# Larger K and V transfers (4 MB items in 32 KB packets), a ring moved to the front of SBUF, regrouped wo loads and late bias loads in a cached-attention decode block

## The chip, the cores and the metric

The kernel runs on one core of a Trainium2 chip. Times are device microseconds of one execution.

The names in the profiles: PE is the matrix engine (PEld its weight loads), DVE the vector engine, ACT the scalar engine, POOL the general one; SP only issues transfers here. A q after a name is the engine's sequencer, which issues its instructions. Data come from the device's memory (HBM) into SBUF, the on-chip memory that the kernel addresses as 128 partitions, by 16 DMA engines (the trace has 16 landings for each item of the stream), in packets; PE writes its results to PSUM. A semaphore is a counter that the trace shows raised when an engine's work, or a transfer, is done.

## The reference, cut to what matters

One decode step for 2 sequences: an attention block with a KV cache, then an MLP, both scaled and shifted by factors computed from a condition c (adaLN). Nearly everything is reading: K and V caches of 2 x 4 x 32,768 x 128 bf16 are 134 MB of the 178 MB.

```python
mod = (_silu(c) @ w_mod).reshape(c.shape[0], 6, 1, -1)        # w_mod 1024 x 6144
sa, ca, ga, sb, cb, gb = ...
h = _layernorm(x) * (1 + ca) + sa
x = x + ga * _A_ref(h, K, V, wq, wo)      # 32 query heads, 4 KV heads, 32768 cached rows
h = _layernorm(x) * (1 + cb) + sb
x = x + gb * _B_ref(h, w1, b1, w2, b2)    # layernorm, 1024 -> 3584, gelu, 3584 -> 1024
```

## The kernel before

All large inputs go through one stream of DMAs, issued in a fixed order by the SP queue. Their target is a ring of 160 KB per partition. A new item may be issued when the items whose bytes it overwrites have been consumed. K and V come in items of 2 MB: 8,192 cache rows, so 64 rows or 16 KB for each of the 128 partitions. V runs five items behind K.

```python
CH_ROWS = 8192
TPC = CH_ROWS // 128          # 64 cache rows per partition and item
VLAG = 5
RING = 160 * 1024
...
    # about 44 KB per partition of small tensors are allocated first, the ring last
    arena = nc.alloc_sbuf_tensor("arena", [128, RING], mybir.dt.uint8)
    abase = nc.lookup_mloc(arena).addr
...
    def add(key, shape, src):                 # next place in the ring
        off = stream[-1].off + stream[-1].nbytes
        if off + nbytes > RING:
            off = 0
        it.view = nc.alloc_sbuf_tensor_at(..., [128] + list(shape), BF16, offset=abase + off)

    for k in range(8):  add(("wmod", k), [6 * DM], ...)       # 12 KB per partition
    for k in range(4):  add(("wq", k), [2, HQ * D], ...)      # 2 x 8 KB
    for n in range(NK + VLAG):
        if n < NK:
            add(("K", n), [TPC, D], kv_src(A_k_cache, ...))   # 16 KB
        v = n - VLAG
        if v >= 0:
            add(("V", v), [TPC, D], kv_src(A_v_cache, ...))
            if v % (2 * NCH) == 2 * NCH - 1:
                add(("wo", g), [8, DM], ...)                  # 16 KB, four of them
    for k in range(4):  add(("w1", k), [2, F], ...)           # 2 x 7 KB
    for k in range(4):  add(("w2", k), [hi - lo, 4 * DM], ...)  # 8 KB each

    def need(*key):                           # issue all items up to this one
        while pos[0] <= it.n:
            cur = stream[pos[0]]
            old = [o.reg for o in stream[:cur.n] if ...overlaps in the ring...]
            T.dma("sp", ..., writes=[cur.reg], frees=old)
```

PE transposes K in groups of 8 rows (`psKT`), DVE and ACT copy to `KT_sb`, PE forms scores and later multiplies V (`psO`). The biases b1 and b2 are loaded at the start from the ACT queue.

## Time and profile before

| | before |
|---|---|
| time, median (runs) | 431.43 us (431.33 to 431.49, 4 runs) |
| span of the profiled run | 429.7 us |
| bytes read | 178.28 MB |
| stream packets on each of the 16 DMA engines | 792, of which 512 are K and V |
| instruction fetches (packets of 16 KB) | 47 |

The page of before: busy time by engine, and the span in 40 slices with the DMA engines' busy share in tenths and the rate.

```profile
span 429.7 us, 12974 instructions
...
PE 292.2 (68%) x6035; PEld 258.2 (60%) x6035; DVE 162.5 (38%) x344; ACT 158.9 (37%) x266; POOL 1.3 (0%) x9
...
DMA  8999999999999999999999999999999999999992
GB/s 332 432 422 426 433 432 424 432 424 427 427 432 427 426 433 429 427 433 426 426 432 426 430 433 424 429 432 426 429 429 428 430 429 424 435 424 424 427 386 112
...
q1 hardware_dynamic: 14112, 178.27, 97.6%
q8 instruction: 47, 0.77, 0.6%
```

No compute engine is near full, and the DMA row is full. q1 is the stream, q8 the fetches of instructions. The chain of waits says the same in its shares of the span:

```profile
DMA 70%; PE 24%; ACT 2%; DVE 2%; issue 1%; SPq 1%; ACTq 0%
```

Now the tail: three windows (start and end in us, their length, busy time and count for each engine, the granted clock, the DMA share, GB/s).

```profile
380.00:410.00 30.00, 16.12 (x309) 12.48 (x310) 6.28 (x32) 1.69 (x3) 0.00 (x0) 0.50 1.01 425
410.00:418.00 8.00, 2.80 (x93) 2.63 (x90) 0.87 (x4) 0.25 (x1) 0.00 (x0) 0.50 0.94 396
418.00:424.00 6.00, 2.56 (x90) 2.48 (x91) 0.00 (x0) 0.00 (x0) 0.00 (x0) 0.50 0.50 208
```

From 418 us on exactly half of the DMA share remains. The landings explain it: the semaphore of an item is raised once by each of the 16 DMA engines, and the trace has each raise. These are the times in us after the first, worked out from the trace for the first and the last item:

```
wmod 0, first landing   6.31:  0  .08 .13 .14 .15 .16 .28 .29 .30 .30 .31 .32 .37 .38 .39 .40
w2 3,   first landing 416.68:  0  .22 .23 .24 .25 .99 1.73 2.84 7.06 7.11 8.53 8.56 8.67 8.70 8.79 9.01
```

Five engines are done at 417 us, three shortly after, and eight only after 423.7 us. The chain of waits in order of time (start, length, what) follows the last landing, at 425.69 us, and then four microseconds of tail:

```profile
396.29 29.40 DMA w<-in_B_w_dram
425.69 0.05 issue
425.74 1.03 PE psS L591 x32
```

A stream packet of 7 KB took 272 ns, of 8 KB 309 and of 16 KB 611, in nearly every case to the nanosecond. A fetch took 945 ns in the mean, and the first stream packet after it 1.09 us instead of 611 ns. So a fetch delays its DMA engine by about 945 + 480 ns, or 1.42 us (an estimate from these means). This is the step: six engines end about six steps late, two about five.

### The profile page before, as it was taken

How to read it: one execution, taken by the hardware profiler on the slowest of the kernel's cores; microseconds unless marked ns; L12 is line 12 of the kernel's file. 1: busy time of each engine (PE TensorE's matmuls, PEld its weight loads, DVE VectorE, ACT ScalarE, POOL GpSimd, SP SyncE). 2: the span in 40 equal slices, each digit the busy share in tenths (PEclk: the TensorE clock that was granted, in tenths of full speed). 3: DMA queues.
4: the chain of work that ended last, by engine and by line, in shares of the span. 5: the costliest groups of instructions: out<-in, count | busy, mean ns of one | idle time of the engine just before them, and what ended most of it. 6: DMA issues, size and time to landing. Idle time of an engine off the chain costs nothing.

```text
span 429.7 us, 12974 instructions
## 1 busy us (share of the span) xinstructions
PE 292.2 (68%) x6035; PEld 258.2 (60%) x6035; DVE 162.5 (38%) x344; ACT 158.9 (37%) x266; POOL 1.3 (0%) x9
## 2 busy tenths in 40 slices
PE   0643379859978764997877649777777697535553
PEld 0632379858867663896757548667666585203543
DVE  0200027545665332463543435445434454203200
ACT  1100016575574325362833534446436343500100
POOL 1000000000000000000000000000000000000000
PEclk9999999998989867696996959986988599555555
DMA  8999999999999999999999999999999999999992
GB/s 332 432 422 426 433 432 424 432 424 427 427 432 427 426 433 429 427 433 426 426 432 426 430 433 424 429 432 426 429 429 428 430 429 424 435 424 424 427 386 112
DMA packets 14500, 179.11 MB, mean 417 GB/s; under 512 B 1767, under 2 KB 1774, under 8 KB 2798
## 3 DMA queue, kind: packets, MB, share of 16 engines
q1 hardware_dynamic: 14112, 178.27, 97.6%
q8 instruction: 47, 0.77, 0.6%
q10 hardware_dynamic: 334, 0.02, 0.1%
q14 instruction: 7, 0.06, 0.0%
HBM read 178.28 MB, written 0.00 MB: 415 GB/s over the span
## 4 chain that ended last, share of the span: by engine, by line
DMA 70%; PE 24%; ACT 2%; DVE 2%; issue 1%; SPq 1%; ACTq 0%
DMA K<-in_A_k_cache_dram 50%; PE psKT L546 15%; DMA V<-in_A_v_cache_dram 9%; DMA w<-in_B_w_dram 7%; DMA wmod<-in_w_mod_dram 5%; PE psS L441 4%; PE psO L473 2%; PE psM L510 1%; ACT E_sb L462 1%; SPq L344 1%; PE psM L494 0%; DVE KT_sb L552 0%; PE psM L483 0%; ACT L462 0%; DVE msum L488 0%
## 5 line engine op out<-in xcount | busy, mean ns | idle before, releaser
L546 PE MATMUL psKT<-ident,K 128*128 128x128 bf16 x2048 | 181.1, 240 | 55.1 <-DMA K<-in_A_k_cache_dram 54.2
L546 PEld LDWEIGHTS psKT<-ident,K 128*128 128x128 bf16 x2048 | 138.2, 108 | 70.0 <-DMA K<-in_A_k_cache_dram 63.5
L550 ACT ACTIVATE KT_sb<-psKT 128x1024 bf16<-128x1024 bf16 x96 | 98.3, 1024 | 190.2 <-PE psKT L546 181.3
L552 DVE COPY KT_sb<-psKT 128x1024 bf16<-128x1024 bf16 x160 | 108.2, 689 | 137.7 <-PE psKT L546 137.0
L441 PE MATMUL psS<-qT,KT_sb 128*128 128x8 bf16 x2048 | 91.6, 168 | 7.2 <-ACT KT_sb L550 4.5
L441 PEld LDWEIGHTS psS<-qT,KT_sb 128*128 128x128 bf16 x2048 | 84.0, 100 | 8.6 <-ACT KT_sb L550 4.9
L473 PE MATMUL psO<-V,E_sb 128*32 128x512 bf16 x512 | 38.2, 424 | 10.1 <-DMA V<-in_A_v_cache_dram 9.5
L462 ACT ACTIVATE E_sb<-S_sb,negm 128x256 bf16<-128x256 f32 x64 | 32.5, 508 | 7.0 <-DVE negm L460 5.2
L447 DVE TENSOR_REDUCE m1c<-S_sb 128x8 f32<-128x512 f32 x32 | 22.0, 688 | 14.1 <-ACT S_sb L446 13.0
L473 PEld LDWEIGHTS psO<-V,E_sb 128*32 128x32 bf16 x512 | 11.5, 101 | 22.3 <-DMA V<-in_A_v_cache_dram 13.3
L446 ACT ACTIVATE S_sb<-psS 128x512 f32<-128x512 f32 x32 | 19.0, 594 | 4.4 <-PE psS L441 4.3
L418 PE MATMUL psS<-siluT,wmod 128*128 128x2 bf16 x384 | 11.2, 165 | 8.4 <-DMA wmod<-in_w_mod_dram 6.9
L418 PEld LDWEIGHTS psS<-siluT,wmod 128*128 128x128 bf16 x384 | 10.9, 104 | 8.8 <-DMA wmod<-in_w_mod_dram 7.3
L426 PE MATMUL psS<-hT,wq 128*128 128x2 bf16 x256 | 7.5, 165 | 12.5 <-DMA wq<-in_A_wq_dram 12.5
L426 PEld LDWEIGHTS psS<-hT,wq 128*128 128x128 bf16 x256 | 7.1, 104 | 12.8 <-DMA wq<-in_A_wq_dram 12.8
L591 PE MATMUL psS<-gT,w 128*128 128x2 bf16 x224 | 6.6, 165 | 9.2 <-DMA w<-in_B_w_dram 9.2
L395 ACT ACTIVATE stat<-stat 128x2 f32<-128x2 f32 x3 | 0.6, 203 | 31.8 <-DVE stat L394 31.8
L591 PEld LDWEIGHTS psS<-gT,w 128*128 128x128 bf16 x224 | 6.3, 104 | 9.5 <-DMA w<-in_B_w_dram 9.5
L462 ACT ACTIVATION_READ_ACCUMULATOR E_sb<-S_sb,negm 128x1 f32 x64 | 12.0, 187 | 0.0
L485 DVE RECIPROCAL rinv<-psM 128x1 f32<-128x1 f32 x8 | 1.3, 168 | 22.1 <-PE psM L483 22.1
L573 PE MATMUL psS<-h2T,w 128*128 128x2 bf16 x224 | 7.8, 172 | 2.5 <-DVE x1b L577 1.3
L573 PEld LDWEIGHTS psS<-h2T,w 128*128 128x128 bf16 x224 | 7.6, 118 | 2.6 <-issue 2.6
(86 smaller groups left out, 93.3 us busy)
## 6 DMA issues: line engine op xcount, KB each, us to landing
K<-in_A_k_cache_dram SPq DMA_DIRECT2D x32, 2048.0 KB, 44.2
V<-in_A_v_cache_dram SPq DMA_DIRECT2D x32, 2048.0 KB, 43.2
wmod<-in_w_mod_dram SPq DMA_DIRECT2D x8, 1536.0 KB, 17.2
wq<-in_A_wq_dram SPq DMA_DIRECT2D x4, 2048.0 KB, 37.7
wo<-in_A_wo_dram SPq DMA_DIRECT2D x4, 2048.0 KB, 43.0
w<-in_B_w_dram SPq DMA_DIRECT2D x4, 1792.0 KB, 41.8
w<-in_B_w_dram SPq DMA_DIRECT2D x3, 2048.0 KB, 31.0
w<-in_B_w_dram SPq DMA_DIRECT2D x1, 1024.0 KB, 29.4
```

Of the source, the lines that this page charges most:

```text
L418: pe(lambda e, w=it.view, j=j, k=k: e.matmul(psS[0][:, 2 * j:2 * j + 2], lhsT=w[:, j * 128:(j + 1) * 128], rhs=siluT[:, :, k], start=(k == ...
L426: pe(lambda e, w=it.view, h=h, k=k: e.matmul(psS[1][:, 2 * h:2 * h + 2], lhsT=w[:, k % 2, h * 128:(h + 1) * 128], rhs=hT[:, k, :], start=( ...
L441: pe(lambda e, t=t, jj=jj: e.matmul(ps[:, t * HPG:(t + 1) * HPG], lhsT=KT_sb[kn][:, jj, :], rhs=qT[:, b, g * HPG:(g + 1) * HPG], start=Tru ...
L446: act(lambda e: e.activation(Sc, ps[:, :].rearrange("p (t h) -> p h t", h=HPG), ACT.Copy), reads=[preg], writes=[f"S_sb{i % 2}_{cc}"])
L447: dve(lambda e: e.tensor_reduce(m1c[:, :, cc], Sc, AX.X, ALU.max), reads=[f"S_sb{i % 2}_{cc}"], writes=[f"m1c{cc}"])
L462: act(lambda e, h=h: e.activation(E_sb[j][:, :, h, :], S_sb[j][:, h, :].rearrange("p (u t) -> p u t", t=4), ACT.Exp, bias=negm[j][:, h:h + ...
L473: pe(lambda e, t4=t4, tg=tg, q=q: e.matmul(psO[32 * q:32 * q + 32, :], lhsT=E_sb[j][:, tg // 4, :, :].rearrange("p h t -> p (h t)"), rhs=i ...
L546: pe(lambda e, kq=kq, jj=jj, w=it.view, t=t: e.transpose(psKT[kq][:, jj * 128:(jj + 1) * 128], w[:, t, :], ident[:, :]), reads=[it.reg, "i ...
L550: act(lambda e, kn=kn, src=src: e.activation(KT_sb[kn][:, :, :], src, ACT.Copy), reads=[f"psKT{kq}"], writes=[f"KT_sb{kn}"])
L552: dve(lambda e, kn=kn, src=src: e.tensor_copy(KT_sb[kn][:, :, :], src), reads=[f"psKT{kq}"], writes=[f"KT_sb{kn}"])
L573: pe(lambda e, w=it.view, fc=fc, q=q, j=j, k=k: e.matmul(psS[0][:, 2 * fc:2 * fc + 2], lhsT=w[:, k % 2, q * 512 + j:(q + 1) * 512:4], rhs= ...
L591: pe(lambda e, w=it.view, q=q, j=j, k=k: e.matmul(psS[1][:, 2 * k:2 * k + 2], lhsT=w[:, q % 2, j * DM + k * 128:j * DM + (k + 1) * 128], r ...
```

## The change

The intent: fewer and larger packets and items for the same bytes, K and V in 4 MB items, whose 128 cache rows for each partition make one packet of 32 KB; "a 1 KB aligned ring"; wo in one item of 4 MB and two of 2 MB; b1 and b2 on the stream's own queue, late. The core of the diff (small consequences for counters, score buffers and schedule steps are cut):

```diff
-CH_ROWS = 8192
+CH_ROWS = 16384
-VLAG = 5
+STEPS = TPC // 8
+VLAG = 2
...
+    arena = nc.alloc_sbuf_tensor("arena", [128, RING], mybir.dt.uint8)
+    abase = nc.lookup_mloc(arena).addr
+    assert abase % 64 == 0
+
     ident = sb("ident", [128, 128], BF16)
...
-    arena = nc.alloc_sbuf_tensor("arena", [128, RING], mybir.dt.uint8)
-    abase = nc.lookup_mloc(arena).addr
...
-            if v % (2 * NCH) == 2 * NCH - 1:
-                g = v // (2 * NCH)
-                add(("wo", g), [8, DM], ...)
+            if v == 4 * NCH - 1:
+                add(("wo", 0), [2, 8, DM], ...)
+    for g in (2, 3):
+        add(("wo", g), [1, 8, DM], ...)
...
-    T.dma("act", ... b1m ...)
-    T.dma("act", ... b2m ...)
+    need("w1", 3)
+    T.dma("sp", ... b1m ...)          # transposed by PE after w1
+    need("w2", 2)
+    for lo, hi in ((0, 3), (3, 8)):
+        T.dma("sp", ... b2m[lo:hi] ...)   # transposed by PE before the last w2 part
```

Before, the ring starts at byte 61,440 of each partition, which is 60 x 1,024. After, it is allocated first and starts at 16,512: behind 128 bytes of constants, 128 past a multiple of 1 KB. The assertion only asks for a multiple of 64.

More of the change, by code (lines that the diff above doesn't have):

```diff
@@ L236, in bass_adaLN_cond__gqa_block_cached__mixer_channel_mlp__decode_kernel @@
     b1T = sb("b1T", [128, FT])
-    b2T = sb("b2T", [128, KT8])
     sgT = sb("sgT", [128, 2, KT8])
@@ L248, in bass_adaLN_cond__gqa_block_cached__mixer_channel_mlp__decode_kernel @@
     qT = sb("qT", [128, 2, HQ], BF16)
-    atT = [sb(f"atT{i}", [128, 8, 2], BF16) for i in range(2)]
+    atT = [sb(f"atT{i}", [128, 8, 2], BF16) for i in range(G)]
     msum = sb("msum", [128, 128])
@@ L263, in bass_adaLN_cond__gqa_block_cached__mixer_channel_mlp__decode_kernel @@
     res16 = sb("res16", [16, 128], BF16)
-    m1c = sb("m1c", [128, HPG, NCH])
+    m1c = sb("m1c", [128, HPG, NT // 64])
     m1 = sb("m1", [128, HPG])
@@ L322, in bass_adaLN_cond__gqa_block_cached__mixer_channel_mlp__decode_kernel @@
             add(("V", v), [TPC, D], kv_src(A_v_cache, v // NCH, v % NCH))
-            if v % (2 * NCH) == 2 * NCH - 1:
-                g = v // (2 * NCH)
-                add(("wo", g), [8, DM], A_wo[g * 1024:(g + 1) * 1024, :].rearrange("(p j) n -> p j n", j=8))
+            if v == 4 * NCH - 1:
+                add(("wo", 0), [2, 8, DM], A_wo[0:2048, :].rearrange("(g p j) n -> p g j n", g=2, j=8))
+    for g in (2, 3):
+        add(("wo", g), [1, 8, DM], A_wo[g * 1024:(g + 1) * 1024, :].rearrange("(g p j) n -> p g j n", g=1, j=8))
     for k in range(4):
@@ L339, in need @@
             old = [o.reg for o in stream[:cur.n] if o.off < cur.off + cur.nbytes and cur.off < o.off + o.nbytes]
-            if len(cur.view.shape) == 3:
-                dst = cur.view[:, :, :]
-            else:
-                dst = cur.view[:, :]
+            dst = cur.view[tuple(slice(None) for _ in cur.view.shape)]
             T.dma("sp", lambda e, dst=dst, src=cur.src: e.dma_start(dst, src), key=f"d_{cur.reg}", writes=[cur.reg], frees=old)
@@ L359, in bass_adaLN_cond__gqa_block_cached__mixer_channel_mlp__decode_kernel @@
     T.dma("act", lambda e: e.dma_start(x16[:, :], A_x.rearrange("b o (k p) -> (b o k) p", p=128)), key="ld_x", writes=["x16"])
-    T.dma("act", lambda e: e.dma_start(b1m[:, :], B_b1.rearrange("(q r) -> q r", r=512)), key="ld_b1", writes=["b1m"])
-    T.dma("act", lambda e: e.dma_start(b2m[:, :], B_b2.rearrange("(k p) -> k p", p=128)), key="ld_b2", writes=["b2m"])
     for t, nm in ((ident, "ident"), (identf, "identf")):
@@ L372, in bass_adaLN_cond__gqa_block_cached__mixer_channel_mlp__decode_kernel @@
     pe(lambda e: e.matmul(psM[:, 0:16], lhsT=x16[:, :], rhs=ident[0:16, 0:16], start=True, stop=True),
-       reads=["x16", "ident"], writes=["psM"], mark=False)
-    for j in range(4):
-        pe(lambda e, j=j: e.matmul(psM[:, 16 + 7 * j:23 + 7 * j], lhsT=b1m[:, j::4], rhs=ident[0:7, 0:7], start=True, stop=True),
-           reads=["b1m", "ident"], writes=["psM"], mark=False)
-    pe(lambda e: e.matmul(psM[:, 44:52], lhsT=b2m[:, :], rhs=ident[0:KT8, 0:KT8], start=True, stop=True),
-       reads=["b2m", "ident"], writes=["psM"])
+       reads=["x16", "ident"], writes=["psM"])
     dve(lambda e: e.tensor_copy(xT.rearrange("p k b -> p b k"), psM[:, 0:16].rearrange("p (b k) -> p b k", b=2)), reads=["psM"], writes=["xT"])
-    dve(lambda e: e.tensor_copy(b1T.rearrange("p (q j) -> p j q", j=4), psM[:, 16:44].rearrange("p (j q) -> p j q", j=4)), reads=["psM"], writes=["b1T"])
-    dve(lambda e: e.tensor_copy(b2T[:, :], psM[:, 44:52]), reads=["psM"], writes=["b2T"])
     def kb(ap2):
@@ L437, in qk @@
         b, g = i % 2, i // 2
-        ps, preg = psS[n % 2], f"psS{n % 2}"
+        hh, half = cc * (TPC // 64) + g8 // 8, (g8 // 8) % 2
+        ps, preg = psS[half], f"psS{half}"
         for jj in range(8):
-            t = g8 * 8 + jj
+            t = (g8 % 8) * 8 + jj
             pe(lambda e, t=t, jj=jj: e.matmul(ps[:, t * HPG:(t + 1) * HPG], lhsT=KT_sb[kn][:, jj, :], rhs=qT[:, b, g * HPG:(g + 1) * HPG],
@@ L443, in qk @@
                reads=[f"KT_sb{kn}", "qT"], writes=[preg], mark=(jj == 7))
-        if g8 == TPC // 8 - 1:
-            Sc = S_sb[i % 2][:, :, cc * TPC:(cc + 1) * TPC]
-            act(lambda e: e.activation(Sc, ps[:, :].rearrange("p (t h) -> p h t", h=HPG), ACT.Copy), reads=[preg], writes=[f"S_sb{i % 2}_{cc}"])
-            dve(lambda e: e.tensor_reduce(m1c[:, :, cc], Sc, AX.X, ALU.max), reads=[f"S_sb{i % 2}_{cc}"], writes=[f"m1c{cc}"])
+        if g8 % 8 == 7:
+            Sc = S_sb[i % 2][:, :, hh * 64:(hh + 1) * 64]
+            act(lambda e: e.activation(Sc, ps[:, :].rearrange("p (t h) -> p h t", h=HPG), ACT.Copy), reads=[preg], writes=[f"S_sb{i % 2}_{hh}"])
+            dve(lambda e: e.tensor_reduce(m1c[:, :, hh], Sc, AX.X, ALU.max), reads=[f"S_sb{i % 2}_{hh}"], writes=[f"m1c{hh}"])
     def softmax_1(i):
-        dve(lambda e: e.tensor_reduce(m1[:, :], m1c[:, :, :], AX.X, ALU.max), reads=[f"m1c{cc}" for cc in range(NCH)], writes=["m1"])
+        dve(lambda e: e.tensor_reduce(m1[:, :], m1c[:, :, :], AX.X, ALU.max), reads=[f"m1c{hh}" for hh in range(NT // 64)], writes=["m1"])
     def softmax_2(i):
@@ L463, in softmax_3 @@
                                             accum_out=rowsum[j][:, h:h + 1]),
-                reads=[f"S_sb{j}_{cc}" for cc in range(NCH)] + [f"negm{j}"], writes=[f"E_sb{j}", f"rowsum{j}"])
+                reads=[f"S_sb{j}_{hh}" for hh in range(NT // 64)] + [f"negm{j}"], writes=[f"E_sb{j}", f"rowsum{j}"])
     def pv(v):
@@ L492, in extract_2 @@
         b, g = i % 2, i // 2
-        at = atT[g % 2]
+        at = atT[g]
         pe(lambda e: e.matmul(psM[:, 256:384], lhsT=hmat.rearrange("p h e -> p (h e)"), rhs=msum[:, :], start=True, stop=True),
@@ L502, in red @@
                 return e.tensor_reduce(at[:, :, b], pick.rearrange("p e j -> p j e"), AX.X, ALU.add)
-        dve(red, reads=["pick"], writes=[f"atT{g % 2}_{b}"])
+        dve(red, reads=["pick"], writes=[f"atT{g}_{b}"])
     def wo(g):
-        it = need("wo", g)
-        at = atT[g % 2]
+        it, gg = (need("wo", 0), g) if g < 2 else (need("wo", g), 0)
+        at = atT[g]
         for j in range(8):
             for k in range(KT8):
-                pe(lambda e, j=j, k=k: e.matmul(psM[:, 400 + 2 * k:402 + 2 * k], lhsT=it.view[:, j, k * 128:(k + 1) * 128], rhs=at[:, j, :],
+                pe(lambda e, j=j, k=k: e.matmul(psM[:, 400 + 2 * k:402 + 2 * k], lhsT=it.view[:, gg, j, k * 128:(k + 1) * 128], rhs=at[:, j, :],
                                                 start=(j == 0 and k == 0), stop=(j == 7), skip_group_check=True),
-                   reads=[it.reg, f"atT{g % 2}_0", f"atT{g % 2}_1"], writes=["psM"], mark=(j == 7 and k == KT8 - 1))
+                   reads=[it.reg, f"atT{g}_0", f"atT{g}_1"], writes=["psM"], mark=(j == 7 and k == KT8 - 1))
         pv_ = psM[:, 400:416].rearrange("p (k b) -> p k b", b=2)
@@ L532, in bass_adaLN_cond__gqa_block_cached__mixer_channel_mlp__decode_kernel @@
         at(n + 1, 2, lambda i=i: extract_2(i))
-        if i % 2:
-            at(n + 1, 6, lambda i=i: wo(i // 2))
+        if i == 3:
+            at(n + 1, 6, lambda: wo(0))
+            at(n + 1, 8, lambda: wo(1))
+        elif i == 5:
+            at(NK + VLAG, 5, lambda: wo(2))
+        elif i == 7:
+            at(n + 1, 6, lambda: wo(3))
     for n in range(NK + VLAG + 1):
-        for g8 in range(TPC // 8):
+        for g8 in range(STEPS):
             if n < NK:
@@ L567, in bass_adaLN_cond__gqa_block_cached__mixer_channel_mlp__decode_kernel @@
     dve(lambda e: e.tensor_copy(h2T[:, :, :], xc[:, :, :]), reads=["xc"], writes=["h2T"])
+    need("w1", 3)
+    T.dma("sp", lambda e: e.dma_start(b1m[:, :], B_b1.rearrange("(q r) -> q r", r=512)), key="ld_b1", writes=["b1m"])
     for k in range(KT8):
@@ L576, in bass_adaLN_cond__gqa_block_cached__mixer_channel_mlp__decode_kernel @@
                reads=[it.reg, "h2T"], writes=["psS0"], mark=(fc == FT - 1))
-    dve(lambda e: e.tensor_tensor(x1b[:, :, :], mod(5), b2T[:, :].unsqueeze(2).to_broadcast([128, KT8, 2]), ALU.mult), reads=["modT", "b2T"], writes=["x1b"])
-    dve(lambda e: e.tensor_tensor(x1b[:, :, :], x1b[:, :, :], x1T[:, :, :], ALU.add), reads=["x1b", "x1T"], writes=["x1b"])
+    for j in range(4):
+        pe(lambda e, j=j: e.matmul(psM[:, 16 + 7 * j:23 + 7 * j], lhsT=b1m[:, j::4], rhs=ident[0:7, 0:7], start=True, stop=True),
+           reads=["b1m", "ident"], writes=["psM"], mark=(j == 3))
+    dve(lambda e: e.tensor_copy(b1T.rearrange("p (q j) -> p j q", j=4), psM[:, 16:44].rearrange("p (j q) -> p j q", j=4)), reads=["psM"], writes=["b1T"])
     dve(lambda e: e.tensor_tensor(zT[:, :, :], psS[0][:, 0:2 * FT].rearrange("p (f b) -> p f b", b=2), b1T[:, :].unsqueeze(2).to_broadcast([128, FT, 2]), ALU.add),
@@ L585, in bass_adaLN_cond__gqa_block_cached__mixer_channel_mlp__decode_kernel @@
     dve(lambda e: e.tensor_tensor(gT[:, :, :], sg[:, :, :], zT[:, :, :], ALU.mult), reads=["sg", "zT"], writes=["gT"])
+    need("w2", 2)
+    b2_v = B_b2.rearrange("(k p) -> k p", p=128)
+    for lo, hi in ((0, 3), (3, 8)):
+        T.dma("sp", lambda e, lo=lo, hi=hi: e.dma_start(b2m[lo:hi, :], b2_v[lo:hi, :]), key=f"ld_b2_{lo}", writes=[f"b2m_{lo}"])
+    need("w2", 3)
     for q in range(7):
         it = need("w2", q // 2)
+        if q == 6:
+            pe(lambda e: e.matmul(psM[:, 44:52], lhsT=b2m[:, :], rhs=ident[0:KT8, 0:KT8], start=True, stop=True),
+               reads=["b2m_0", "b2m_3", "ident"], writes=["psM"])
+            dve(lambda e: e.tensor_tensor(x1b[:, :, :], mod(5), psM[:, 44:52].unsqueeze(2).to_broadcast([128, KT8, 2]), ALU.mult),
+                reads=["modT", "psM"], writes=["x1b"])
+            dve(lambda e: e.tensor_tensor(x1b[:, :, :], x1b[:, :, :], x1T[:, :, :], ALU.add), reads=["x1b", "x1T"], writes=["x1b"])
         for j in range(4):
```

## The prediction

> **What bounds the kernel now.** The DMA stream. The page: span 429.7 us, 178.3 MB read, DMA at 9 tenths in nearly all 40 slices, 422 to 435 GB/s in the middle; PE is busy for 68%, DVE 38%, ACT 37%. The chain of waits is 70% DMA. By the issue and landing times, 12 to 19 MB are queued ahead at every issue after the start: the stream never starves, and the SP queue's waits on PE (197 us) are only the ring being full.
>
> The averages hide a second part. The windows of the tail give a DMA share of 0.94 for 410 to 418 us and 0.5 from 418 to 424. The 16 landings of one item lie 0.4 us apart for the first item and 9.0 us for the last: some engines finish 9 us late. The lag grows in steps of about 1.42 us that go with the 47 instruction-fetch packets of 16 KB (945 ns each, and the next stream packet takes about 1.1 us instead of 611 ns). Six engines collect six such steps. These end the kernel: last landing 425.7 us, then 4 us of tail.
>
> **What the change does to that.**
> 1. 32 KB packets: K and V go from 512 packets on each engine to 256. On the leading engine, 2 MB items of 16 packets (wq, w2) land 4.88 to 4.90 us apart, those of 8 packets (K, V) 4.86: about 3.4 ns per packet. [...] 256 fewer: 0.9 us.
> 2. 33 fewer items: 33 fewer semaphore packets on each engine, 9 ns each: 0.3 us.
> 3. Instruction fetches: the same 6,013 PE instructions are built, so the same fetches and lag. [...] Gain 0; here nearly 9 us stay.
> 4. b1 and b2 leave the start. Their packets take 18 and 46 ns on at most 8 engines, and the lag at 14 us is still under 0.5 us: gain 0. Late, they hide beside waits for w2: cost 0.
> 5. Ring: five 4 MB slots instead of ten of 2 MB. K0 lands 5 us later and slots come free later, but even when PE runs behind (11 to 14 us for 4 MB of K), nearly 4 items (about 39 us) stay queued. Cost 0.
> 6. wo 2 and 3 come after all of V; wo 3 lands where it did. LayerNorm, w1 and GELU end about 1 us before w2 lands; this stays.
> 7. Alignment: as built, the ring starts at byte 61,440 (a multiple of 1 KB) before and 16,512 (128 bytes past one) after. No gain; a loss of 0 to 2 us is possible.
>
> **Predicted time.** 431.4 - 1.2 = 430.2 us, range 428.7 to 431.8. Chances: faster by over 2%: 0.02; within 2%: 0.96; slower: 0.02.
>
> **What would show each step.** 4,096 packets of 32 KB, about 1,213 ns each, in place of 8,192 of 16 KB. Leading-engine landings 9.69 us apart per 4 MB, not 2 x 4.86. Still 47 fetches, a spread of about 9 us at the end, and half the DMA share in the last 8 us. At least 8 MB ahead at each issue; no middle slice under 420 GB/s.
>
> **What would make it wrong.** A fetch between 32 KB packets that costs much more or less than 1.42 us (six times on the late engines); a penalty of the new ring address; slower HBM reads with partition rows 32 KB apart; a starved queue in the K-only beginning, where PE falls behind.

The sum is 0.9 us (step 1) and 0.3 us (step 2), 1.2 us in all, and 0 for the other steps.

## The result, and the profile after

| | before | after |
|---|---|---|
| time, median | 431.43 us (431.33 to 431.49, 4 runs) | 432.75 us (432.70 to 432.88, 4 runs) |
| ratio | | 1.0031 (95%: 1.0014 to 1.0049) |
| span of the profiled run | 429.7 us | 430.9 us |
| first and last landing of the last item | 416.68, 425.69 us | 417.21, 427.00 us |

A ratio is the mean time of one kernel's runs over that of the other's runs of the same rounds, so it is not quite the ratio of the medians. Executions over 1.5% slower than the fastest of the same kernel are left out of the means.

The change makes the kernel slower by 0.3%. That lies within 2%, but outside the predicted range and on the other side of the kernel before. The page after, and the chain's shares:

```profile
span 430.9 us, 12949 instructions
...
PE 286.8 (67%) x6035; PEld 257.1 (60%) x6035; DVE 161.2 (37%) x343; ACT 157.5 (37%) x266; POOL 1.3 (0%) x9
...
DMA  8999999999999999999999999999999999999982
GB/s 330 428 421 420 439 433 433 423 425 429 431 424 429 421 432 438 430 432 424 422 424 427 440 435 420 427 423 433 433 432 424 428 428 426 424 416 418 419 367 113
...
q1 hardware_dynamic: 9518, 178.27, 97.2%
q8 instruction: 47, 0.77, 0.7%
...
DMA 65%; PE 26%; ACT 4%; DVE 2%; issue 1%; SPq 1%; DVEq 0%; ACTq 0%
```

4,594 packets are gone from q1 and the stream is still full: its bound has not moved. The number of fetches is the same, 47, but their share rose from 0.6 to 0.7%. The three windows of the tail:

```profile
380.00:410.00 30.00, 16.90 (x367) 13.34 (x360) 6.21 (x31) 1.69 (x3) 0.00 (x0) 0.61 1.01 419
410.00:418.00 8.00, 3.87 (x122) 3.69 (x119) 1.07 (x5) 0.25 (x1) 0.00 (x0) 0.50 0.96 397
418.00:424.00 6.00, 1.87 (x64) 1.79 (x64) 0.00 (x0) 0.00 (x0) 0.00 (x0) 0.50 0.54 224
```

From 380 to 410 us, where wo, w1 and w2 run in both kernels with the same packets, the rate fell from 425 to 419 GB/s at the same DMA share of 1.01. No engine starved: the packets got longer. The chain's end is the same, 1.3 us later:

```profile
398.35 28.65 DMA w<-in_B_w_dram
427.00 0.05 issue
427.04 1.03 PE psS L602 x32
```

The single packets show what happened. Means in ns, without those that follow a fetch; the spread is the last minus the first of the 16 landings of the last item:

| | ring at | 7 KB | 8 KB | 16 KB | 32 KB | fetch | spread, us |
|---|---|---|---|---|---|---|---|
| before | 61,440 | 272.0 | 309.0 | 611.0 | | 945 | 9.01 |
| after | 16,512 | 276.0 | 313.3 | 614.7 | 1,216.5 | 1,066 | 9.78 |

Packets of 7, 8 and 16 KB take about 4 ns longer, those of w1 and w2 too, which the change did not touch. The 12 KB packets of wmod, the first of the stream, take only 1.4 ns longer in the mean (461.8 against 460.3), and the first half of them are not longer at all. Fetches take 0.12 us longer in the mean, even the first two (1,059 ns; before 932 and 929), which run beside 12 KB packets of wmod before any 32 KB packet exists. That spoke against the packet size and for the ring's address, but one trace of a change with four parts does not show it.

### The profile page after: what moved, and what is told of

The parts are those of the page before. It is cut to its first block, busy times and chain, and to the rows that moved or that the text cites. A ratio compares the mean times of both kernels' runs of the same rounds, so it can differ in the third digit from the quotient of the medians.

```text
span 430.9 us, 12949 instructions
## 1 busy us (share of the span) xinstructions
PE 286.8 (67%) x6035; PEld 257.1 (60%) x6035; DVE 161.2 (37%) x343; ACT 157.5 (37%) x266; POOL 1.3 (0%) x9
## 4 chain that ended last, share of the span: by engine, by line
DMA 65%; PE 26%; ACT 4%; DVE 2%; issue 1%; SPq 1%; DVEq 0%; ACTq 0%
DMA K<-in_A_k_cache_dram 45%; PE psKT L542 16%; DMA wo<-in_A_wo_dram 9%; DMA w<-in_B_w_dram 7%; DMA wmod<-in_w_mod_dram 5%; PE psS L432 5%; ACT E_sb L453 3%; PE psO L464 2%; PE psM L501 1%; DVE KT_sb L548 1%; SPq L343 1%; ACT KT_sb L546 1%; PE psM L485 1%; PE psM L474 1%; PE psM L444 0%
## 5 line engine op out<-in xcount | busy, mean ns | idle before, releaser
L542 PE MATMUL psKT<-ident,K 128*128 128x128 bf16 x2048 | 178.2, 238 | 45.1 <-DMA K<-in_A_k_cache_dram 43.7
L542 PEld LDWEIGHTS psKT<-ident,K 128*128 128x128 bf16 x2048 | 136.0, 107 | 53.9 <-DMA K<-in_A_k_cache_dram 46.8
L464 PE MATMUL psO<-V,E_sb 128*32 128x512 bf16 x512 | 34.7, 417 | 6.6 <-ACT E_sb L453 5.5
L464 PEld LDWEIGHTS psO<-V,E_sb 128*32 128x32 bf16 x512 | 13.2, 104 | 21.2 <-issue 10.9
L501 PE MATMUL psM<-atT,wo 128*128 128x2 bf16 x256 | 7.1, 164 | 3.7 <-DMA wo<-in_A_wo_dram 3.7
L501 PEld LDWEIGHTS psM<-atT,wo 128*128 128x128 bf16 x256 | 6.9, 99 | 3.9 <-DMA wo<-in_A_wo_dram 3.9
```

The lines of the kernel that those rows point to most:

```text
L464: pe(lambda e, t4=t4, tg=tg, q=q: e.matmul(psO[32 * q:32 * q + 32, :], lhsT=E_sb[j][:, tg // 4, :, :].rearrange("p h t -> p (h t)"), rhs=i ...
L501: pe(lambda e, j=j, k=k: e.matmul(psM[:, 400 + 2 * k:402 + 2 * k], lhsT=it.view[:, gg, j, k * 128:(k + 1) * 128], rhs=at[:, j, :], start=( ...
L542: pe(lambda e, kq=kq, jj=jj, w=it.view, t=t: e.transpose(psKT[kq][:, jj * 128:(jj + 1) * 128], w[:, t, :], ident[:, :]), reads=[it.reg, "i ...
```

## The experiments

Three theories. **A**: the ring's address, 128 bytes past a multiple of 1 KB, makes every packet and every fetch dearer, and the larger packets are in themselves a gain. **B**: larger packets or items make a fetch dearer. **C**: the regrouped wo and the late b1 and b2 cost the time. All runs passed the check of their results (which let an omission in e3 pass, see there); the tables give medians, and the kernel before as it ran in the same rounds.

### e1: the kernel before with its ring 128 bytes further

```diff
     # the kernel before, nothing else changed
+    nc.alloc_sbuf_tensor("ring_pad", [128, 128], mybir.dt.uint8)
     arena = nc.alloc_sbuf_tensor("arena", [128, RING], mybir.dt.uint8)
```

Expected: 

> The kernel before with nothing changed but 128 bytes of padding ahead of the ring, so that it starts at 61,568, 128 bytes past a multiple of 1 KB. Theory A (ring address): every stream packet gets about 3 to 5 ns longer (7 KB packets from 272 to about 277 ns in the mean, 16 KB from 611 to about 614 in the median), a fetch goes from 945 to about 1,066 ns, the final spread from 9.0 to about 9.9 us, and the time rises by 2.5 to 3.5 us to 434 to 435 us (about 3 ns on 1,050 packets of each engine, and 6 x 0.15 us of fetches). Theory B (32 KB packets or larger items make a fetch dearer): no change, 431.4 us, fetch 945 ns. Theory C (wo regrouped, b1 and b2 late cost the time): no change.

Measured: 435.19 us against 431.42 us, ratio 1.0087 (1.0073 to 1.0101). Packets of 7 KB 276.1 ns, of 16 KB 614.3 ns, fetches 1,065 ns, spread 9.78 us. The window that fell from 425 to 419 GB/s in the change reads the same here:

```profile
380.00:410.00 30.00, 15.69 (x261) 10.69 (x253) 6.29 (x32) 1.69 (x3) 0.00 (x0) 0.50 1.00 419
```

So 128 bytes of padding alone, with packets, items and program unchanged, give both marks of the change and cost 3.8 us, a little more than the 2.5 to 3.5 us expected. B and C are refuted as causes of these two marks. The last item's first landing is 2.87 us later, over 792 packets 3.6 ns for each; the spread adds 0.77 us.

### e2: the change with its ring on a multiple of 1 KB

```diff
     # the kernel after
+    nc.alloc_sbuf_tensor("ring_pad", [128, 896], mybir.dt.uint8)
     arena = nc.alloc_sbuf_tensor("arena", [128, RING], mybir.dt.uint8)     # now at 17,408
```

Expected: 

> The kernel after with 896 bytes of padding ahead of the ring, which then starts at 17,408, a multiple of 1 KB. Theory A: packets of 7 KB back at 272 ns and of 32 KB at 1,213 ns, fetch back at 945 ns, spread about 9.0 us, time about 430.2 us, my prediction for the change without an alignment cost. Theory B: packets back at their length, but fetch still 1,066 ns and spread 9.9 us: about 431.1 us. Theory C: 432.7 us as after, less what shorter packets give.

Measured: 429.90 us (429.80 to 430.17), ratio to before 0.9966 (0.9953 to 0.998). Packets are back at 272, 309 and 611 ns, those of 32 KB take 1,213 ns, a fetch 936 ns, the spread is 8.92 us.

```profile
span 428.1 us, 12949 instructions
```

and its windows of the tail:

```profile
380.00:410.00 30.00, 17.08 (x400) 14.78 (x400) 6.83 (x34) 1.69 (x3) 0.00 (x0) 0.61 1.01 425
410.00:418.00 8.00, 3.04 (x107) 2.96 (x108) 0.45 (x3) 0.25 (x1) 0.00 (x0) 0.50 0.86 359
418.00:424.00 6.00, 2.69 (x92) 2.50 (x89) 0.16 (x1) 0.00 (x0) 0.00 (x0) 0.50 0.45 187
```

The rate in the first window is 425 GB/s again. The intended version beats both kernels: 1.5 us under before and 2.85 us under the change as it was built. (The kernel after ran in other rounds; by the ratios to before, 1.0031 and 0.9966, the difference is 2.8 us.) 2.85 us agrees with the trace: the last landing comes at 424.19 instead of 427.00 us, of which the first landing makes 1.95 us (536 packets, again 3.6 ns each) and the spread 0.86 us, most of which is six fetches of 0.13 us each.

### e3: e2 with K and V in 2 MB items again

```diff
     # e2
-CH_ROWS = 16384
+CH_ROWS = 8192
-VLAG = 2
+VLAG = 5
```

(and the score buffer chosen by the item's number again).

Expected: 

> As e2, with K and V again in 2 MB items of 16 KB packets (ten slots, V five items behind), so that of the change only the wo grouping, the late b1 and b2 and the moved tensors remain. Theory A: within 0.3 us of before, 431.4 us, and 1.2 us slower than e2. Theory B: fetch back at 945 ns only here, time 431.4 us and equal to or faster than e2. Theory C: over 431.4 us, by what wo, b1 and b2 cost.

Measured: 431.41 us, ratio to before 0.9998 (0.9986 to 1.0011); fetch 931 ns.

One thing is wrong with this run, and the check of the results did not notice it. The change puts the product with the second wo group at step 8 of an item. An item of 2 MB has only steps 0 to 7, so in e3 this product is never computed, although its weights are loaded. The trace shows three products of 64 matmuls instead of four (e2 first, then e3):

```profile
L502 PE MATMUL psM<-atT,wo x256: 163/163/185, 260.2 to 391.6; 128*128 128x2 bf16 x128
L502 PE MATMUL psM<-atT,wo x192: 163/165/187, 261.2 to 392.9; 128*128 128x2 bf16 x192
```

That takes 64 matmuls out of the middle, and one fetch (46 in place of 47). The bytes and transfers are complete, and the last item's eight late landings come in the same steps as before (7.07 and 7.23 us, six from 8.56 to 8.69), so the omission should not have moved the end; a run with the fourth product was not made.

With this reserve, what remains of the change, wo regrouped, b1 and b2 late, tensors moved, is worth nothing that these runs can tell. e2, which computes everything, says the same: of its 1.52 us under before, the closer landings of K and V explain 1.4 (worked out in the point on steps 1 and 2). C falls, and B too: with 2 MB items (e3) and with 4 MB items (e2) a fetch costs the same. e3 minus e2 is what the large items are worth: 1.51 us.

### e4, e5, e6: how much alignment it takes

The kernel before with 64, 256 and 512 bytes of padding ahead of its ring, otherwise as e1.

Expected of 64 bytes: 

> The kernel before with 64 bytes of padding ahead of the ring (61,504). If only the remainder by some power of two counts, whether 256, 512 or 1,024: the same loss as with 128 bytes, fetch about 1,066 ns, 435 us. If the loss grows with the distance: half of it, about 433.3 us. If 64 bytes are alignment enough: 431.4 us and fetch 945 ns.

Expected of 256 bytes: 

> The same with 256 bytes (61,696). If a multiple of 256 is enough: 431.4 us, 7 KB packets 272 ns, fetch 945 ns. If 512 or 1,024 is needed: about 435 us as with 128 bytes.

Expected of 512 bytes: 

> The same with 512 bytes (61,952). If a multiple of 512 is enough: 431.4 us, fetch 945 ns. If 1,024 is needed: about 435 us.

| padding | ring start modulo 256 | time, us | before, us | ratio (95%) | 7 KB packet, ns | fetch, ns |
|---|---|---|---|---|---|---|
| 64 (e4) | 64 | 435.35 | 431.31 | 1.0094 (1.0078 to 1.0111) | 276.3 | 1,076 |
| 128 (e1) | 128 | 435.19 | 431.42 | 1.0087 (1.0073 to 1.0101) | 276.1 | 1,065 |
| 256 (e5) | 0 | 431.35 | 431.31 | 1.0001 (0.9987 to 1.0016) | 272.0 | 936 |
| 512 (e6) | 0 | 431.41 | 431.31 | 1.0005 (0.999 to 1.002) | 272.0 | 931 |

Here a ring on a multiple of 256 lost nothing (e5, e6), one 64 or 128 bytes past it lost 0.9% (e4, e1), and between these two the loss doesn't grow with the distance (4.04 and 3.77 us). The assertion in the change would pass in each of the four cases.

### e8: the smallest repair of the change

```diff
     # the kernel after; the ring then starts at 16,640 = 65 x 256
+    nc.alloc_sbuf_tensor("ring_pad", [128, 128], mybir.dt.uint8)
```

Expected: 

> The kernel after with only 128 bytes of padding, so that the ring starts at 16,640, a multiple of 256 but not of 512. If a multiple of 256 is all that is needed, with 32 KB packets too: as e2, 429.9 us, 32 KB packets 1,213 ns, fetch about 940 ns. If the large packets need 1 KB: over 431 us.

Measured: 430.11 us (before 431.39 us, ratio 0.997, 0.9955 to 0.9985), 32 KB packets 1,213 ns, fetch 943 ns. So 256 is enough for the large packets too, which took 1,216.5 ns at 16,512.

### e7: six more fetches, a test that failed

The sums above rest on the reading that the late engines are late because of instruction fetches. To test it, I added useless matmuls among those of wq, each of them two PE instructions (a weight load and a multiply); they write unused PSUM.

```diff
     # e2, in the wq loop, eight times
+        for r in range(96):
+            pe(lambda e: e.matmul(psM[:, 500:502], lhsT=ident[:, :], rhs=hT[:, 0, :], start=True, stop=True), ...)
```

Expected: 

> e2 (the change on a 1 KB aligned ring) with 768 useless small matmuls among those of wq, where PE has time; they write an unused part of PSUM and the result stays right. They are 1,536 more PE instructions, 6 more fetches (53 in place of 47). If the lag of the late engines is made of fetches, and the late engines end the kernel: half of the late engines get one more step, spread from 8.9 to about 10.3 us, time from 429.9 to about 431.3 us. If the lag has another cause, or PE's fetches do not end the kernel: no change, 429.9 us.

Measured: 437.30 us (before 431.31 us), 53 fetches, but a spread of 7.38 us. The test was not clean. The matmuls took more time than I had reckoned: K began at 84.4 us instead of 63.2 us, PE freed the ring's slots late, and the stream ran empty.

```profile
100.00:120.00 20.00, 16.77 (x390) 16.04 (x387) 12.34 (x22) 12.75 (x21) 0.00 (x0) 1.00 1.00 418
120.00:140.00 20.00, 16.99 (x364) 15.16 (x368) 10.48 (x16) 12.18 (x20) 0.00 (x0) 0.83 0.68 279
```

The DMA share of 0.68 in the second window is the gap. While the stream waited, the late engines caught up (the spread fell from 3.3 us to about 0.5 us for all but one), so the end says nothing of fetches. It does show how much room the five-slot ring has: PE 21 us late in the K-only beginning is too much.

### e9: three more fetches, in PE's idle time

Half as many useless matmuls, 32 after each wmod item and 16 after each half of a wq item.

Expected: 

> e2 with 384 useless small matmuls (half of e7), 32 after each wmod item and 16 after each half wq item, so that K starts as in e2 (at about 63 us; in e7 it started 21 us late and the ring ran empty). 768 more PE instructions, 3 more fetches (50). If fetches make the lag and the late engines end the kernel: one to three engines get a seventh step, spread from 8.9 to about 10.3 us, time from 429.9 to about 431.3 us. If not: 429.9 us and spread 8.9 us.

Measured: 431.24 us (431.14 to 431.30; before 431.39 us in these rounds, 431.42 us in those of e2), 50 fetches: 768 instructions made three more, one for each 256, as 1,536 made six in e7. K began at 63.2 us as in e2, and the stream stayed full.

```profile
q8 instruction: 50, 0.82, 0.7%
```

The landings of the last item in us after the first:

```
e2, first 415.26:  0 .14 .18 .30 .31 .32 2.26 3.07  7.14 7.46  8.54 8.59 8.71 8.82 8.84  8.92
e9, first 415.48:  0 .04 .09 .10 .13 .30 1.74 2.45  8.28 8.45  8.46 8.47 8.50 8.60 8.67  9.98
```

The two engines with five steps got their sixth, and one with six its seventh. This one alone ends the kernel: the last landing is 1.27 us later (0.22 in the first landing, 1.06 in the spread) and the time 1.34 us, about one step. e2 ran on another chip; against e8, which differs from e2 only in the padding and ran in the same rounds as e9, it is 1.13 us. So fetches make the lag, and the latest engine sets the time. The packet records name no DMA engine; that the fetches fall on eight of the 16 in turn is read from these landings, and from the fetches' durations, which repeat in eights: before, 932, 929, 967, 968, 947, 886, 881, 941 ns, then 933, 921, 962, 961, 949, 886, 886, 941.

## Why the prediction was wrong, point by point

- **Step 7, alignment, is the step that failed.** It said: "No gain; a loss of 0 to 2 us is possible." Measured, the loss is 2.85 us (432.75 us as built, 429.90 us in e2 with only the padding changed; 2.64 us against e8). I had read both addresses from the builds, and then left the term out of the sum: 430.2 us is the time without it, and the upper end of 431.8 us did not even hold the 2 us that the step itself allowed. Those 2 us were a guess: no run had moved the ring yet.
- **Step 3, fetches: "Gain 0".** It took the cost of a fetch to be unaffected by the change, which no run had shown. True for the packets' size: with 32 KB packets on an aligned ring a fetch takes 936 ns (931 to 945 beside 16 KB in e3, e5, e6 and before) and the spread is 8.92 us (e2). Not true for the address: 1,066 ns, and 0.86 us more at the end. This is about 0.3 of the loss, and I had not thought of any link between the ring's address and fetches.
- **Steps 1 and 2, the gain of larger packets and fewer semaphores,** were right in direction and somewhat small: 1.2 us estimated, 1.51 us measured between e3 and e2, 1.52 us between before and e2. The landings of K and V on the leading engine (the first of the 16 to finish an item) are 9.68 us apart per 4 MB in e2, against 2 x 4.863 us before: about 0.044 us less, 32 times, or 1.4 us. I had forecast 9.69. The kernel after, with its longer packets, has 9.71. The runs show the gain of fewer packets and fewer semaphores in sum alone, not each by itself.
- **Step 4, b1 and b2, and step 6, wo:** 0, as predicted, as far as the runs can tell. e3, which keeps their transfers, is within 0.02% of before, but lacks one of the four wo products; e2 has them all and leaves 0.1 us that the landings of K and V don't explain.
- **Step 5, the ring:** at least 8.4 MB were queued ahead at each issue after the first few, as predicted under the marks (8), but that is two items and at most about 20 us of transfers, not the "nearly 4 items (about 39 us)" of the step itself: it fell so low at five issues, first at 105.8 us. The stream did not starve, and the middle slices stay at 420 GB/s or more. (Single slices are a rough mark: some of e2 read 416 too. The windows of the tail are the better one.) e7 shows that the room is not large.
- Of the predicted marks, the 4,096 packets of 32 KB, the 47 fetches and the half share at the end came true; the time of a packet (1,213 ns) came true only in e2.

In one sum, in us: 431.4 (before) - 1.5 (large items) + 2.85 (ring address) = 432.75. It closes by construction, since both terms are differences to e2; what supports it from outside is that e1, without large items, shows the same 3.6 ns per packet and nearly the same growth of the spread.

Not settled: why a destination off a multiple of 256 lengthens packets of 7 to 32 KB by about 4 ns (3.5 to 4.3) whatever their size, but the first 12 KB packets of wmod not at all, and why it lengthens a fetch (945 to 1,066 ns), which the trace has on a queue of its own (q8), apart from the stream (q1). The runs show that both go with the ring's address and with nothing else that was changed (e1 moves the ring alone; in e5 and e6 the padding alone costs nothing).

## What to carry to other kernels

In this kernel, bound by its DMA stream, moving a buffer by 128 bytes changed the time (3.8 us in e1) and not only the place: check the built address of every streamed buffer, and align it (here to 256 bytes per partition) rather than assert something weaker. Read the landings of one item over all 16 engines, not the mean rate: here the mean rate hides that eight engines finish 7 to 9 us late, and what lengthens the latest counts in full (e9: last landing 1.27 us later, time 1.34 us). And put each risk that can be read off the build into the sum, or test it, before trusting a gain of a fraction of a per cent. When an experiment changes a constant on which a schedule depends, count the instructions in its trace: e3 passed its check with a product missing.
